# Loading q in memory order, half B first in the last batch, and norms placed by GpSimd's readiness: one change to a fused BigBird attention and FNet kernel

## The chip, the cores and the metric

The program runs on one core of a Trainium2 chip. The time is the device time of one launch in microseconds (us), given as the median of several executions. The span of a profiled execution is about 2 us shorter than its time; where the text takes numbers from the inside of a trace, it speaks of the span. In the traces PE is TensorE's matmuls and PEld its weight loads, DVE is VectorE, ACT ScalarE, POOL GpSimd and SP SyncE; SPq and ACTq are the queues of instructions of these engines, from which transfers are issued. PSUM is the memory that TensorE writes to. The granted clock is the share of TensorE's full clock that the trace recorded, 1.00 or 0.50 at any moment and a mean over a stretch.

## The reference, cut to what matters

Attention for 4 batches of 8 heads, 768 positions of 64 values each, under a block mask that is the same for all heads. Its output, as 768 rows of 512 per batch, goes through a two-dimensional Fourier mix, a normalisation of each row and two matrix products.

```python
scores = scale * np.matmul(q, k.transpose(0, 1, 3, 2))
...                                  # band, first/last block, three sampled blocks a row
attn = np.exp(scores - max); attn = attn / (sum + 1e-09)
x = attn @ v                         # (B, H, S, D) -> (B, S, H*D)
mixed = np.real(np.fft.fft(np.fft.fft(x, axis=1), axis=2))
u  = x + mixed
un = (u - mean(u)) / np.sqrt(var(u) + 1e-06)
out = u + np.maximum(un @ w_ch1, 0.0) @ w_ch2
```

## The kernel before

Heads are worked in 16 pairs, and each pair in six slots. In a slot TensorE computes two blocks of scores, ScalarE takes their exponentials, and TensorE multiplies the exponentials of the slot before with v. In between come the transposes of the next pair's q and k, the rounding of the weights (which arrive as 64-bit numbers in 32 chunks), and from the second batch on the matmuls of the batch before. Every engine executes its instructions in the order in which they were emitted.

The 768 positions are kept in an order that suits the Fourier mix: rows walk up and down in steps of two. `_ORDER` describes it, and `_rows` turns each entry of it into one or more pieces of a transfer. Before the change q was put into this order by the loads themselves, so that a pair needs 18 of them:

```python
    def load_q(dst, b, h, n, tiles=range(C), queues=None):
        queues = queues or [nc.sync]
        for t in tiles:
            if t < T:
                for p0, cnt, rows in _rows(q[b, h], t, ((S * D, n),)):
                    queues[0].dma_start(out=dst[p0:p0 + cnt, t, 0:n, :], in_=rows)
                continue
            for i in range(n):
                for p0, cnt, rows in _rows(q[b, h + i], t):
                    queues[i % len(queues)].dma_start(out=dst[p0:p0 + cnt, t, i, :], in_=rows)
```

A half of q (or k) is then transposed and copied out of PSUM by one instruction:

```python
    def turn(n, a, half):
        ...
        for c in range(T):
            nc.tensor.transpose(tp[:, c * P:(c + 1) * P], t[:, T * half + c, :, :], ident)
        if n == 0 and a == 0:
            nc.vector.tensor_copy(out=dst[:, half * HS:(half + 1) * HS], in_=tp[:, 0:HS])
        else:
            nc.scalar.copy(out=dst[:, half * HS:(half + 1) * HS], in_=tp[:, 0:HS])
```

At the end of a batch the halves A (0) and B (1) of the rows follow one another. Each tile of 128 rows is added by VectorE and stored; `_rows` gives two stores of 64 rows for the last tile of half A, and one of 2 x 64 rows for the last tile of half B:

```python
            nc.vector.tensor_tensor(out=x[:, m, :], in0=y, in1=x[:, m, :], op=ALU.add)
            for p0, cnt, rows in _rows(out[b], T * half + m):
                nc.sync.dma_start(out=rows, in_=x[p0:p0 + cnt, m, :])
    ...
        for half in range(2):
            rest += [lambda half=half, f=f: hidden(half, f) for f in range(NF)]
            rest += [lambda half=half, m=m, p=p: channels(half, m, p) ...]
```

A last part, `with tc.If(over > 0): general()`, is a slow way for large inputs. It is never executed with these inputs, but its branch is.

## Time and profile before

| what | kernel before |
|---|---|
| time, median of 3 runs | 1183.69 us |
| profiled span | 1180.5 us |
| TensorE busy | 1134.4 us |
| ScalarE busy | 364.8 us |
| issues of q loads by SyncE and by ScalarE | 278 and 10 (16 pairs of 18) |

Two more readings. First, the windows of slots 1 and 2. The columns are the stretch, its length, busy time (and count) of PE, PEld, DVE, ACT and POOL, the granted clock, DMA share and GB/s.

```profile
15.28:29.30 14.02, 8.75 (x32) 2.60 (x32) 0.56 (x1) 2.72 (x6) 0.00 (x0) 0.88 0.40 107
29.30:35.85 6.55, 6.55 (x31) 2.15 (x31) 3.79 (x7) 5.07 (x9) 0.00 (x0) 0.73 0.64 225
```

Second, the row of groups for the copies of q out of PSUM on ScalarE (busy us and mean ns behind the bar): 30 copies of 384 columns.

```profile
L448 ACT COPY qT<-tp 128x384 f32<-128x384 f32 x30 | 14.3, 478 | 65.3 <-PE tp L443 65.3
```

### The profile page before, as it was taken

What the parts mean: (1) busy time and instruction counts of PE and PEld (TensorE: products, weight loads), DVE (VectorE), ACT (ScalarE), POOL (GpSimd) and SP (SyncE); (2) the same over time, 40 slices, a digit from 0 to 9 for tenths busy, and PEclk for the clock granted to TensorE, in tenths of its full rate; (3) what the DMA queues carried; (4) which work ended last, traced back from release to release, by engine and by line L of the source; (5) the groups of instructions that cost most, each with busy time, mean ns of one, the idle gap of its engine ahead of it and who ended that gap; (6) DMA issues with size and microseconds to landing.
All of it is one profiled execution on the core that took longest, in us unless ns stands there. A gap on an engine that the chain in (4) does not pass through costs nothing.

```text
span 1180.5 us, 11884 instructions
## 1 busy us (share of the span) xinstructions
PE 1134.4 (96%) x4412; PEld 542.6 (46%) x4412; DVE 413.5 (35%) x751; ACT 364.8 (31%) x672; POOL 245.7 (21%) x181
## 2 busy tenths in 40 slices
PE   5999998989999999999999999999999999999996
PEld 1333333434654555455444555454444554554542
DVE  2787889487201433022224743022232223000000
ACT  1876765445200321144323331044321211100100
POOL 0000057457100311043333421033331001000000
PEclk9998999989999999999999999999999999999998
DMA  5546511111000100010101000001000000000000
GB/s 141 169 127 216 179 40 46 36 35 37 1 6 24 25 1 9 31 29 26 29 23 45 14 14 3 29 23 27 1 18 9 1 1 19 9 5 23 0 10 20
DMA packets 65281, 44.26 MB, mean 37 GB/s; under 512 B 52902, under 2 KB 58048, under 8 KB 65216
## 3 DMA queue, kind: packets, MB, share of 16 engines
q1 hardware_dynamic: 62576, 42.44, 12.6%
q10 hardware_dynamic: 2640, 0.98, 0.3%
q8 instruction: 37, 0.61, 0.2%
q14 instruction: 28, 0.23, 0.1%
HBM read 37.11 MB, written 6.29 MB: 37 GB/s over the span
## 4 chain that ended last, share of the span: by engine, by line
PE 88%; DVE 4%; ACT 2%; DMA 2%; issue 1%; SPq 1%; POOL 0%; ACTq 0%; DVEq 0%; POOLq 0%
PE hp L796 28%; PE y L810 28%; PE s L468 10%; PE o L510 9%; PE tp L443 2%; DVE e L489 2%; PE zp L670 1%; PE zp L681 1%; PE sp L557 1%; PE utp L786 1%; DMA qr<-in_q_dram 1%; PE xt L528 1%; PE s L473 1%; DMA wraw<-in_moe_w_ch_dram 1%; PE sp L571 1%
## 5 line engine op out<-in xcount | busy, mean ns | idle before, releaser
L796 PE MATMUL hp<-unT,w_sb 128*128 128x384 f32 x1024 | 341.4, 487 | 0.7 <-ACT unT L787 0.7
L810 PE MATMUL y<-w_sb,hs 128*128 128x512 f32 x768 | 337.6, 593 | 0.0
L796 PEld LDWEIGHTS hp<-unT,w_sb 128*128 128x128 f32 x1024 | 190.5, 190 | 131.1 <-issue 4.2
L498 POOL TENSOR_TENSOR acc<-acc,e 128x768 f32<-128x768 f32 x96 | 178.3, 1857 | 315.4 <-DVE e L489 311.2
L810 PEld LDWEIGHTS y<-w_sb,hs 128*128 128x128 f32 x768 | 142.8, 190 | 169.6 <-issue 168.6
L489 DVE TENSOR_TENSOR e<-s,mask 128x768 f32<-128x768 f32 x144 | 131.1, 951 | 249.5 <-ACT s L487 249.5
L468 PE MATMUL s<-qT,kT 64*128 64x384 f32 x768 | 165.5, 538 | 14.6 <-ACT e L484 8.0
L798 ACT ACTIVATE hs<-hp 128x384 f32<-128x384 f32 x128 | 62.7, 490 | 357.9 <-PE hp L796 357.9
L510 PE MATMUL o<-e,vr 128*64 128x384 f32 x768 | 149.5, 511 | 0.0
L487 ACT ACTIVATE s<-s 128x768 f32<-128x768 f32 x144 | 108.8, 793 | 91.4 <-PE s L468 90.7
L815 DVE TENSOR_TENSOR x<-y,x 128x512 f32<-128x512 f32 x24 | 16.6, 691 | 336.3 <-PE y L810 336.3
L468 PEld LDWEIGHTS s<-qT,kT 64*128 64x128 f32 x768 | 65.4, 192 | 76.2 <-issue 31.1
L496 POOL TENSOR_TENSOR acc<-e 128x768 f32<-128x768 f32 x24 | 44.5, 1856 | 268.2 <-DVE e L489 206.3
L510 PEld LDWEIGHTS o<-e,vr 128*64 128x64 f32 x768 | 47.6, 139 | 77.8 <-issue 74.3
L484 ACT ACTIVATE e<-s 128x768 f32<-128x768 f32 x48 | 36.6, 803 | 19.9 <-DMA qk<-in_q_dram 11.3
L745 POOL TENSOR_SCALAR rstd<-mv 128x1 f32<-128x1 f32 x24 | 6.4, 267 | 152.8 <-DVE mv L743 152.1
L712 DVE TENSOR_TENSOR un<-pq,un 128x255 f32<-128x255 f32 x12 | 5.1, 423 | 88.3 <-ACT un L709 88.3
L787 ACT COPY unT<-utp 128x512 f32<-128x512 f32 x24 | 14.0, 585 | 68.9 <-PE utp L786 68.8
L448 ACT COPY qT<-tp 128x384 f32<-128x384 f32 x30 | 14.3, 478 | 65.3 <-PE tp L443 65.3
L731 DVE TENSOR_TENSOR x<-x,un 128x127 f32<-128x127 f32 x96 | 32.7, 402 | 0.1
L443 PE MATMUL tp<-ident,qr 128*128 128x128 f32 x90 | 18.6, 307 | 9.0 <-DVE sums L541 3.5
L448 ACT COPY kT<-tp 128x384 f32<-128x384 f32 x32 | 15.3, 479 | 32.7 <-PE tp L443 30.1
(142 smaller groups left out, 680.3 us busy)
## 6 DMA issues: line engine op xcount, KB each, us to landing
wraw<-in_moe_w_ch_dram SPq DMA_DIRECT2D x32, 512.0 KB
vr<-in_v_dram SPq DMA_DIRECT2D x30, 192.0 KB
kr<-in_k_dram SPq DMA_DIRECT2D x28, 192.0 KB
qr<-in_q_dram SPq DMA_DIRECT2D x118, 32.0 KB
out_dram<-x SPq DMA_DIRECT2D x16, 128.0 KB
out_dram<-x SPq DMA_DIRECT2D x8, 256.0 KB
qr<-in_q_dram SPq DMA_DIRECT2D x59, 31.5 KB
out_dram<-x SPq DMA_DIRECT2D x8, 126.0 KB
```

The source lines that it names most:

```text
L443: nc.tensor.transpose(tp[:, c * P:(c + 1) * P], t[:, T * half + c, :, :], ident)
L468: nc.tensor.matmul(s[:, i, 0:HS], kT[D * i:D * i + D, c * P:(c + 1) * P], qT[D * i:D * i + D, half * HS:(half + 1) * HS], start=True, stop ...
L484: nc.scalar.activation(out=e, in_=s[:, :, 0:HS], func=ACT.Exp, scale=scale)
L487: nc.scalar.activation(out=s[:, :, 0:HS], in_=s[:, :, 0:HS], func=ACT.Exp, scale=scale)
L489: nc.vector.tensor_tensor(out=e, in0=s[:, :, 0:HS], in1=m.broadcast_to([P, 2, HS]), op=ALU.mult)
L496: nc.gpsimd.tensor_add(out=acc_of[n, half], in0=e_of[u - 1], in1=e)
L498: nc.gpsimd.tensor_add(out=acc_of[n, half], in0=acc_of[n, half], in1=e)
L510: nc.tensor.matmul(o[D * i:D * i + D, :], vt[:, i, c, :], e[:, i, :], start=(c == 0), stop=(c == C - 1))
L731: tt(out=xs, in0=xs, in1=at, op=op)
L796: nc.tensor.matmul(ps[:, 0:T * P], w1_sb[:, d, f * P:(f + 1) * P], unT[half][:, d, :], start=(d == 0), stop=(d == ND - 1))
L798: nc.scalar.activation(out=hs[half, f // 4][:, f % 4, :], in_=ps[:, 0:T * P], func=ACT.Relu)
L810: nc.tensor.matmul(y, hs[half, f // 4][:, f % 4, m * P:(m + 1) * P], w2_sb[:, f, :], start=(f == 0), stop=(f == NF - 1))
```

## The change

It has three parts. q is loaded as it lies in memory, two neighbouring rows to a partition, in 6 loads a pair (96 in all); the copies out of PSUM, now nine a pair, put it in order. The last batch works half B before half A, so that the tile with two plain stores comes last. And a normalisation on VectorE is placed by the scheduler only once GpSimd's reciprocal deviation should be there (`rstd_at`). With the first part, the sampled blocks are loaded by GpSimd in place of SyncE, some loads at the start move, and the transposes of the second pair's q come one slot earlier.

```diff
+_TURNED = (((0, 64, 192, -64, 64, 1), (256, 64, 256, -192, 64, 1), (129, 63, 385, -384, 63, 1),
+            (128, 127, 0, 384, 1, 1), (641, -128, 383, 127, 63, -1), (512, 127, 320, 191, 1, 1)),
+           ((384, 64, 191, 64, 64, -1), (704, -128, 64, 63, 63, -1), (640, 127, 0, 1, 1, 1)))
 ...
+        for t in range(T):
+            for i in range(2):
+                rows = q[b, 2 * j + i][2 * P * t:2 * P * (t + 1), :]
+                nc.sync.dma_start(out=qt[:, t, :, i, :],
+                                  in_=rows.rearrange("(p r) d -> p r d", r=2))
 ...
-    nc.sync.dma_start(out=samp_i.rearrange("a b c -> a (b c)"),
+    nc.gpsimd.dma_start(out=samp_i.rearrange("a b c -> a (b c)"),
 ...
+            copy = nc.vector.tensor_copy if n == 0 else nc.scalar.copy
+            for to, to_jump, frm, jump, cnt, step in _TURNED[half]:
+                copy(out=_grid(dst, to, 2, to_jump, cnt, 1),
+                     in_=_grid(tp, frm, 2, jump, cnt, step))
 ...
+            rstd_at.append(busy("POOL", 0.8, when["DVE"] + HOP) + HOP)
 ...
+                if kind == "w" and rstd_at[0] > max(when["DVE"], when["PE"]) + 0.2:
+                    break
 ...
+        order = (1, 0) if b == B - 1 else (0, 1)
 ...
-        for half in range(2):
+        for half in order:
 ...
-            for at, a, half in (((2, 0, 0), (3, 0, 1), (4, 1, 0), (5, 1, 1)) if n == 0 else
-                                ((1, 0, 0), (2, 0, 1), (4, 1, 0), (5, 1, 1))):
+            for at, a, half in ((1, 0, 0), (2, 0, 1), (4, 1, 0), (5, 1, 1)):
 ...
-        if sl == 0:
-            load_q_half(1, 1, [nc.sync, nc.scalar])
-        if s == (4 if n == 0 else 3) and n + 2 < len(pairs):
-            load_q_half(n + 2, 0)
-            load_q_half(n + 2, 1)
+        if s == 3 and n + 2 < len(pairs):
+            load_q(n + 2)
 ...
+    load_q(1)
     w_load(1)
     load_k(1)
-    load_q_half(1, 0)
-    w_load(2)
 ...
-    load_q_half(0, 1, [nc.sync, nc.scalar])
```

## The prediction

> **What bounds the kernel now.** I read the engine totals and the slices first.
>
> ```profile
> PE 1134.4 (96%) x4412; PEld 542.6 (46%) x4412; DVE 413.5 (35%) x751; ACT 364.8 (31%) x672; POOL 245.7 (21%) x181
> ...
> PE   5999998989999999999999999999999999999996
> ...
> PEclk9998999989999999999999999999999999999998
> ```
>
> TensorE is busy 1134.4 of 1180.5 us, so a change that removes no matmul can win only from the 46.1 us in which TensorE is idle, and from matmuls run at a reduced clock. The table of windows says where the idle time is: 0 to 12 us has 4.39 busy, 12 to 40 has 22.01, 40 to 140 has 94.43, 140 to 280 has 125.47, 280 to 320 has 38.19; then 320 to 1100 is fully busy at clock 1.00, and 1100 to 1181 has 69.91. So nothing between 320 and 1170 us can be gained; the case is decided in the first 320 us and in the last 10.
>
> Second, the list of what TensorE waited for:
>
> ```profile
> PE s L468 <- ACT e L484: 8.0, 3, 4.4
> PE tp L443 <- DMA qr<-in_q_dram: 7.0, 3, 5.4
> PE s L468 <- DVE e L489: 5.6, 6, 1.9
> PE xt L528 <- ACT oT L516: 4.0, 5, 1.0
> PE tp L443 <- DVE sums L541: 3.5, 1, 3.5
> ```
>
> The largest is a wait for ScalarE's exponentials, so third, the timeline shows why ScalarE was late. Twice the cause is the loading of q:
>
> ```profile
> 23.43 4.90 ACTq L199 DMA_DIRECT2D qk<-in_q_dram  x5
> ...
> 28.43 1.51 ACT L484 ACTIVATE e<-s 128x768 f32<-128x768 f32 x2 [11.30 <-DMA qk<-in_q_dram]
> 29.29 0.51 PEld L468 LDWEIGHTS s<-qT,kT 64*128 64x128 f32 x4 [4.58 <-ACT e L484]
> 29.30 1.65 PE L468 MATMUL s<-qT,kT 64*128 64x384 f32 x4 [4.39 <-ACT e L484]
> ```
>
> ScalarE issues five loads of q (23.43 to 28.33) in front of two exponentials whose scores were finished by 19.4; TensorE sits idle 4.39 us, and comes back slow (four score matmuls take 1.65 us; they take 0.92 from 35.9 on).
>
> ```profile
> 84.22 6.03 SPq L199 DMA_DIRECT2D qr<-in_q_dram  x10
> ...
> 90.36 1.63 SPq L402 DMA_DIRECT2D wraw<-in_moe_w_ch_dram  x3
> ...
> 94.98 0.66 ACT L411 ACTIVATE wraw<-wraw 128x512 f32<-128x512 uint32 x1 [4.31 <-DMA wraw<-in_moe_w_ch_dram]
> ...
> 98.22 1.65 PE L468 MATMUL s<-qT,kT 64*128 64x384 f32 x4 [2.88 <-ACT e L484]
> ```
>
> Here SyncE spends 79.28 to 90.25 issuing 18 loads of q (8, then these 10), and the weights queue behind them. ScalarE, which works in order, waits 4.31 us for the weight chunk with exponentials behind it, and TensorE waits 2.88. The slots from 90.0 and 98.2 took 8.2 us each where their neighbours take 5.0 to 5.2, with a granted clock of 0.62 in the second: 16.4 - 10.3 = 6.1 us lost in all.
>
> Last, the end. VectorE's last add ends at 1170.64, the span at 1180.5. By windows of one microsecond (DMA share and GB/s are the last two columns):
>
> ```profile
> 1088.00:1089.00 1.00, 1.00 (x5) 0.60 (x4) 0.16 (x1) 0.00 (x0) 0.00 (x0) 1.00 0.00 0
> 1089.00:1090.00 1.00, 1.00 (x5) 0.60 (x4) 0.00 (x0) 0.00 (x0) 0.00 (x0) 1.00 0.67 154
> 1090.00:1091.00 1.00, 1.00 (x5) 0.60 (x4) 0.00 (x0) 0.49 (x1) 0.00 (x0) 1.00 0.51 115
> ...
> 1173.00:1174.00 1.00, 0.00 (x0) 0.00 (x0) 0.00 (x0) 0.00 (x0) 0.00 (x0) 0.50 0.15 37
> ...
> 1177.00:1178.00 1.00, 0.00 (x0) 0.00 (x0) 0.00 (x0) 0.00 (x0) 0.00 (x0) 0.50 0.13 49
> ```
>
> Both are 256 KB of output. The last tile of half A (two stores of 64 rows) is through about 2.9 us after its add ended at 1088.16; the last of half B (one store of 2 x 64 rows) needs to about 1178.2, 7.6 us, at a DMA share of 0.13 to 0.16, that is two of sixteen engines.
>
> **What the Trainium skill says.** "DMA: Bandwidth & Descriptors", section "Why a DMA increments its semaphore by 16 and not by 1": a transfer uses the largest number of engines up to 16 that divides the slowest dimension of both sides. A destination of 2 x 64 rows gets 2, 64 or 128 rows get 16. The trace agrees: 0.13 to 0.16 is 2/16 and a little. The same holds for the q loads of tiles 3 to 5, and single rows get one engine. Same page, "Issuing engines are not separate DMA queues": issuing from another engine saves only the sequencer's time; here ScalarE's sequencer is the one that pays, 0.98 us a load. "ScalarE: Activation LUTs", "What ACT_TABLE_LOAD costs": an activation costs a fixed 186 ns plus 0.833 ns a column, and neighbours overlap by about 93 ns. The trace is some 28 ns below it: copies of 384, 126 and 2 columns take 478, 263 and 162 ns, and neighbours overlap by 0.1 us. "TensorE: Matmul & The Clock Gate", "What's actually happening": an idle window halves the clock and sustained work restores it. The slices at 26 to 31 us with clock 0.50, and the 1.65 us at 98.22, agree; why the dense stretch from 15.3 to 24 us ran at the slow durations too, the trace does not tell.
>
> **The change part by part.** I also compared the built instruction orders of the two kernels, engine by engine.
>
> *q loads.* 18 issues a pair become 6, all of 128 partitions. At about 0.6 us each (5.00/8, 5.67/10) a pair takes 3.7 us of SyncE for 10.9, and ScalarE issues no q. The weights behind them go out 7 us sooner, more than the 4.31 waited at 90.7, so the 6.1 us there are gained whole.
>
> *The start.* The first scores (9.62) get later. The sampled blocks are now loaded by GpSimd, ahead of its mask work; about 1 us (estimate, from the "~1 µs" first-byte figure for that path in the DMA page's "Specifications", since no GpSimd load is in this trace) delays the mask chain on VectorE, which ends at 9.07. Then VectorE does six copies in place of one: four of about 0.29 (0.558 less 256 columns) and two of 0.15, overlapping, 1.15 us for 0.56. First scores about 11.2. But slot 0 no longer waits for ScalarE (0.73 before), and slot 1 ends near 24.0, as before (24.9). At its end the order has four transposes of pair 1, whose six copies ScalarE must finish before the two of pair 0 can take the only bank: 1.2 + 1.0 wait + 0.5. Slot 2 scores at 26.7 in place of 29.3, 2.6 us won; the clock, not halved by a gap of over 4 us, should give about 0.7 more (0 to 3.4 is possible). The tight transpose after an output transpose near 41 us is moved: 0.5. Sum of the start: 3.8 us.
>
> *Copies out of PSUM.* ScalarE's two copies a pair (0.96 us) become nine: six large at 0.265 and three small at 0.162, 2.08 busy. Over 15 pairs that is +17 us of ScalarE's busy time, 365 to about 382. After overlap the first half costs 0.9 in place of 0.48, the second about 0.5 as before. ScalarE has 1.7 to 1.9 us to spare in the slots that hold the first half (2.99 and 3.16 busy of 4.9 from 127.4 to 137.2), so it is hidden, except where both halves of q are transposed back to back: TensorE's two waits for qT of 0.57 at 166.5 and 259.7 grow by 0.5 each: -1.0.
>
> *Half B first in the last batch.* The last tile is then two stores of 64 rows: 7.6 becomes 2.9, gain 4.7.
>
> *Norms.* In the built orders VectorE's normalisations stand where they stood in batches 0 to 2, and TensorE's order differs by one group of four matmuls. The waits this was meant for (2.34 us for GpSimd at 253.15, behind the 3.55 at 258.19) stay: 0.
>
> Sum: 6.1 + 3.8 + 4.7 - 1.0 = 13.6 us; 1183.69 - 13.6 = 1170.1.
>
> **Rivals.** (1) *ScalarE becomes the bound of the first stage*: the copies go into slots in which ScalarE is already tight (5.29 of 5.9 us from 121.5, 5.32 of 6.0 from 137.2, where TensorE loses 0.97). For it: an in-order engine, 1.1 us more a pair. Against: those slots hold the cheap second half. It would give back about 0.5 us in each of 15 pairs at most, only 8 of them where TensorE is not saturated: 4 us, 1174. (2) *The start is lost, not won*: GpSimd's load is slow or lands late and the mask chain ends several microseconds later. The scores then start at 13 or more and the gain of the start is gone: 1174. (3) *The clock comes up early*: with no gap after the first scores, slots 1 and 2 run warm (slot 1 took 8.2 us of matmuls; its warm work is 4.9), 3.4 us more: 1167. (4) *The norm rule works after all* and removes the 3.5 us at 258: 1167. Against it, the identical order.
>
> **Range and chances.** 1170 us; the terms at 90 us and at the end are read off the trace to a microsecond, the start is uncertain by 3 either way, the rivals by 4. So 1165 to 1176. A 2% gain would need 1160, that is 23.7 us, half of all idle time, and the roughly 16 us between 140 and 320 are not addressed: 0.04. Slower by 2% would need a new stall of over 37 us: 0.01.
>
> **What would show it.** Right: last add to end of span about 5 us; no wait for weights over 2 us before 110 us, and slots of 5.0 to 5.3 there; no q issues by ScalarE; TensorE's work from 320 us on moved as a block. Wrong: first scores after 12 us; ScalarE's exponentials late in the slots with the six copies; the 3.5 us at 258 gone; a tail still near 10 us.

## The result, and the profile after

The changed kernel takes 1164.34 us, median of four runs (1163.42 to 1167.2), beside 1184.41 us of the kernel before on the same chip. The ratio is 0.9834 with a 95% interval of 0.9812 to 0.9856. A ratio here is the mean time of one kernel's runs over that of the other's runs of the same rounds, so it is not quite the ratio of the medians. The predicted 1170 is 5.7 us too long, and the median lies 0.7 us under the low end of the range. Four later executions of the same file, on another occasion, took 1166.31 to 1168.3 us, inside it.

The totals and the clock of the kernel after:

```profile
PE 1124.9 (97%) x4412; PEld 540.4 (47%) x4412; DVE 414.4 (36%) x758; ACT 373.0 (32%) x777; POOL 247.1 (21%) x182
...
PEclk9999999989999999999999999999999999999999
```

The matmuls are the same 4412, so 9.5 us less of busy TensorE is the same work, less of it at the half clock (the mean granted clock over the span goes from 0.987 to 0.994). The rest of the 18.8 us of span is idle time removed, and ScalarE pays 8.2 us for it.

A span can be cut at marks that exist in both traces: the start of slot 4 (its first scores), one transpose of attention output (at 142.66 us before), the first matmul of the hidden layer (`hp`), the end of VectorE's last add, and the end. The table gives each stretch in us, from the timelines of both kernels and of five runs described below.

| profiled run | to slot 4 | slot 4 to the transpose | to the first `hp` | to the end of the last add | tail | span |
|---|---|---|---|---|---|---|
| before | 41.99 | 100.67 | 151.87 | 876.1 | 9.9 | 1180.5 |
| after | 32.81 | 94.80 | 151.86 | 876.1 | 6.1 | 1161.7 |
| after, repeated | 35.09 | 94.75 | 154.32 | 876.1 | 6.1 | 1166.4 |
| q part alone | 35.01 | 94.80 | 154.36 | 876.1 | 9.4 | 1169.7 |
| half B first alone | 41.35 | 100.80 | 151.76 | 876.1 | 6.2 | 1176.2 |
| norms alone | 42.74 | 97.62 | 154.01 | 876.1 | 9.9 | 1180.4 |
| q in 18 pieces | 37.58 | 100.74 | 152.45 | 876.1 | 6.1 | 1173.0 |

Between before and after the stretches differ by 9.2, 5.9, 0, 0 and 3.7 us, in all 18.8. The stretch to the first `hp` takes 151.8 to 154.4 us with and without the change, and the next is always the same; neither belongs to it. (By the clock record the three runs at 151.8 to 151.9 had 10.2 us at half clock in that stretch, those at 154.0 to 154.4 had 13.7 to 17.1.)

The start first. The windows of slots 1 and 2 of the kernel after answer to the two shown of before:

```profile
15.94:23.07 7.13, 6.01 (x35) 2.26 (x35) 0.00 (x0) 4.03 (x12) 0.00 (x0) 1.00 0.99 333
23.07:27.89 4.82, 4.82 (x32) 1.64 (x31) 3.06 (x8) 4.58 (x8) 0.00 (x0) 1.00 0.17 63
```

Slot 1 takes 7.13 us in place of 14.02 and slot 2 takes 4.82 in place of 6.55. How that comes about is in the timeline of TensorE (start, duration, and the idle time before with its releaser):

```profile
11.08 1.65 PE L474 MATMUL s<-qT,kT 64*128 64x384 f32 x4 [2.90 <-DVE qT L452]
...
15.94 1.46 PE L474 MATMUL s<-qT,kT 64*128 64x384 f32 x4
...
17.59 0.92 PE L474 MATMUL s<-qT,kT 64*128 64x384 f32 x4
...
22.70 0.44 PE L444 MATMUL tp<-ident,qr 128*128 128x128 f32 x2 [1.12 <-ACT qT L452]
23.07 0.92 PE L474 MATMUL s<-qT,kT 64*128 64x384 f32 x4
```

Four score matmuls take 1.65 us, then 1.46, then 0.92: the clock rises to full about 17 us, 6 us after the first scores, and stays there. In the kernel before, the same groups still take 1.65 us at 29.30, and 0.92 only from 35.85 on. (One trap: in the windows the clock reads 1.00 before the first change that the trace has recorded, though the matmuls there run at the slow duration. At the start of a trace, read the durations.) Of the wait of 1.12 us at 22.70 the prediction had said 1.0.

Near 70 us SyncE now spends 3.85 us on the q loads of a pair, and the weights follow at 74.38:

```profile
70.44 3.85 SPq L214 DMA_DIRECT2D qr<-in_q_dram  x6
...
74.38 1.49 SPq L400 DMA_DIRECT2D wraw<-in_moe_w_ch_dram  x3
```

ScalarE's rows for the copies, by form, hold nine copies a pair where the row of before held two:

```profile
L452 ACT COPY qT<-tp 128x126 f32<-128x126 f32 x45 | 12.3, 274 | 0.0
...
L452 ACT COPY qT<-tp 128x128 f32<-128x128 f32 x45 | 10.5, 269 | 63.7 <-PE tp L444 63.7
...
L452 ACT COPY qT<-tp 128x2 f32<-128x2 f32 x45 | 7.8, 174 | 0.5
```

They sum to 30.6 us where 14.3 were before, 16.3 more (17 predicted), of which 8.2 remain as busy time because neighbours overlap. In the list of what TensorE waited for, the waits for these copies did grow, and the wait for VectorE's sums is still there:

```profile
PE xt L534 <- ACT oT L522: 4.1, 5, 1.0
...
PE tp L444 <- DVE sums L547: 3.6, 1, 3.6
PE tp L444 <- ACT qT L452: 3.4, 3, 1.1
```

Last the tail. VectorE's last add ends at 1155.56. The windows of one microsecond show the two stores of 64 rows running at a share of 0.85, and the rows of the line that closes the program show what SyncE did meanwhile (duration in ns min/median/max, then first and last start):

```profile
1157.00:1158.00 1.00, 0.00 (x0) 0.00 (x0) 0.00 (x0) 0.00 (x0) 0.00 (x0) 0.56 0.85 195
1158.00:1159.00 1.00, 0.00 (x0) 0.00 (x0) 0.00 (x0) 0.00 (x0) 0.00 (x0) 0.50 0.08 23
```

```profile
L1114 SPq COMPARE_BRANCH  x1: 50/50/50, 1156.8 to 1156.8; - x1
...
L1114 SPq EVENT_SEMAPHORE  x8: 17/17/17, 1159.7 to 1160.2; - x8
```

The data is through about 2.7 us after the add, as predicted (2.9). But SyncE's branch over the unused slow way, begun at 1156.8, lets the next instruction start only at 1159.7: 2.9 us, and that now comes last.

### The profile page after: what moved, and what is told of

Read it like the earlier page. It is cut to its first block, busy times and chain, and to the rows that moved or that the text cites. A ratio compares the mean times of both kernels' runs of the same rounds, so it can differ in the third digit from the quotient of the medians.

```text
span 1161.7 us, 11697 instructions
## 1 busy us (share of the span) xinstructions
PE 1124.9 (97%) x4412; PEld 540.4 (47%) x4412; DVE 414.4 (36%) x758; ACT 373.0 (32%) x777; POOL 247.1 (21%) x182
## 4 chain that ended last, share of the span: by engine, by line
PE 91%; DVE 4%; ACT 2%; issue 1%; POOL 0%; ACTq 0%; POOLq 0%; DVEq 0%
PE hp L808 29%; PE y L822 29%; PE s L474 11%; PE o L516 10%; PE tp L444 2%; DVE e L495 1%; PE zp L676 1%; PE zp L687 1%; PE sp L563 1%; PE s L479 1%; PE xt L534 1%; PE utp L798 1%; PE sp L577 1%; DVE x L737 0%; PE pq L696 0%
## 5 line engine op out<-in xcount | busy, mean ns | idle before, releaser
L474 PE MATMUL s<-qT,kT 64*128 64x384 f32 x768 | 162.4, 529 | 8.9 <-DVE e L495 5.8
L516 PE MATMUL o<-e,vr 128*64 128x384 f32 x768 | 145.9, 501 | 0.0
L452 ACT COPY qT<-tp 128x128 f32<-128x128 f32 (+1 forms) x135 | 22.4, 239 | 64.2 <-PE tp L444 63.7
```

Of the source, the lines that this page charges most:

```text
L474: nc.tensor.matmul(s[:, i, 0:HS], kT[D * i:D * i + D, c * P:(c + 1) * P], qT[D * i:D * i + D, half * HS:(half + 1) * HS], start=True, stop ...
L516: nc.tensor.matmul(o[D * i:D * i + D, :], vt[:, i, c, :], e[:, i, :], start=(c == 0), stop=(c == C - 1))
```

## The experiments

Twelve more runs were made, one of them of the unedited kernel after; all gave correct results. They are told in the order of what they settle.

**The three parts alone.** `q part alone` is the kernel after with the old order of halves and the old norm rule. `Half B first alone` and `norms alone` are the kernel before with one part each.

```diff
# q part alone, against after
-        order = (1, 0) if b == B - 1 else (0, 1)
+        order = (0, 1)
-        wh = [[("w", lambda ...: whiten(half, m), 0.0, 0.0, 0.6) ...
+        wh = [[d(0.6, whiten, half, m) ...
# half B first alone, against before
+        order = (1, 0) if b == B - 1 else (0, 1)
-        for half in range(2):
+        for half in order:
# norms alone, against before
+            rstd_at.append(busy("POOL", 0.8, when["DVE"] + HOP) + HOP)
+                if kind == "w" and rstd_at[0] > max(when["DVE"], when["PE"]) + 0.2:
+                    break
```

> The changed kernel with the first half leading in every batch and the norms placed by the old rule, so the q part alone. Theory A (the gain is the q loads: start 9.3 us, weights near 90 us 5.8 us, read off the two traces): 15 us below the kernel before, 1168 to 1170, the tail from the last add to the end back near 9.9 us. Rival B (the three parts need each other, the norm rule carries part of the middle): 1172 or more.

> The kernel before with half B leading in the last batch and nothing else. Theory A (the tail is the store over two engines, and under it lies SyncE's branch of 2.9 us, so 3.7 us are won and not the predicted 4.7): 1180 to 1181, last add to end 6.1 us, the first 320 us as before. Rival B (the tail is other work, for instance the end of the program): no change, 1184.

> The kernel before with the norm rule alone. Theory A (VectorE's order is the same, so nothing moves): within 1 us of the kernel before, and the wait of 3.5 us for the sums near 258 us stays. Rival B (the rule carries part of the gain in the first 320 us): 1 to 3.5 us faster and that wait shorter.

Measured, beside 1183.23 us of the kernel before: q part 1169.49 us (ratio 0.9869, 0.9843 to 0.9895), half B first 1177.84 (0.9949, 0.9923 to 0.9974), norms 1182.26 (0.999, 0.9959 to 1.0021). The table of stretches shows where: the q part has the two early gains and the long tail, half B first has the short tail and neither of the early gains. Norms alone keeps the whole wait that it was meant for; its line in the waits of TensorE:

```profile
PE tp L443 <- DVE sums L541: 3.5, 1, 3.5
```

So the gain is the q part's and the tail's, and the norm rule gives nothing that these runs resolve. By the medians the parts give 13.7 and 5.4 us, 19.1 in sum; the whole gave 20.1 the first time and 15.7 when it was repeated (below), so that they add up is not contradicted, and not shown more closely than that. Half B first was some 2 us faster than expected; its trace shows 3.7 us in the tail, and the kernel before alone spread from 1180.27 to 1187.69 in these rounds.

**q in 18 pieces.** The kernel after, with the same bytes in the same places but each load cut in three by partitions, brings back the number of issues and nothing else.

```diff
-                nc.sync.dma_start(out=qt[:, t, :, i, :],
-                                  in_=rows.rearrange("(p r) d -> p r d", r=2))
+                rows = rows.rearrange("(p r) d -> p r d", r=2)
+                for p0, p1 in ((0, 48), (48, 96), (96, 128)):
+                    nc.sync.dma_start(out=qt[p0:p1, t, :, i, :], in_=rows[p0:p1])
```

> The changed kernel with each load of q cut into three by partitions (48, 48, 32): 18 issues a pair again, the same bytes and packets, all on 16 engines. Theory A (the weights were late because SyncE spent 11 us issuing q ahead of them): ScalarE's wait for weights comes back, one or two slots over 6 us between 60 and 110 us, 4 to 8 us slower than the changed kernel, 1168 to 1172. Rival B (the weights waited behind q's packets on the two engines that carried them): no such wait, within 1.5 us of the changed kernel.

Measured: 1173.93 us, ratio 0.9912 (0.9888 to 0.9936). The stretch from slot 4 to the transpose is 100.74 us, that of the kernel before, where after has 94.80. Its timeline of SyncE and its list of waits give the chain:

```profile
74.68 11.48 SPq L216 DMA_DIRECT2D qr<-in_q_dram  x18
...
86.26 1.48 SPq L401 DMA_DIRECT2D wraw<-in_moe_w_ch_dram  x3
```

```profile
ACT wraw L410 <- DMA wraw<-in_moe_w_ch_dram: 9.5, 4, 3.8
...
PE s L475 <- ACT e L491: 4.3, 2, 2.7
```

Eighteen issues hold SyncE for 11.48 us, so the weights go out 11.6 us after the first of them and not 3.9; ScalarE waits 3.8 us for a chunk, and TensorE waits 2.7 us for ScalarE and comes back with score groups of 1.65 us. So the count of issues, for the same bytes, brings the 5.9 us back. About half of them is the wait, the other half the slow clock behind it, and the second half need not come: in norms alone, which has the old loads, TensorE waited nearly as long, the clock stayed up, and the stretch took 97.62 us, only 2.8 more than in the kernel after. The first line is from q in 18 pieces, the second from norms alone:

```profile
93.72 1.65 PE L475 MATMUL s<-qT,kT 64*128 64x384 f32 x4 [2.70 <-ACT e L491]
```

```profile
98.79 0.92 PE L468 MATMUL s<-qT,kT 64*128 64x384 f32 x4 [2.61 <-ACT e L484]
```

The time is 2 us over the expected 1168 to 1172: another 2.5 us come at the start, where slot 4 begins at 37.58, not near 35: slot 3 waits 1.63 us for an exponential. This run does not say more of the start.

**The kernel after once more, and the start.** Before the start could be judged, the spread between executions of the same file had to be known.

```diff
# after, repeated: no edit
```

> The changed kernel once more, unedited, beside the variants of this call. It should repeat: 1163 to 1168 us, in two groups some 3 us apart if the moment at which the clock comes up (17 us in its first profile, about 22 in the profile of the q part alone) is what differs between executions.

Measured: 1167.3 us, ratio 0.9861 (0.9839 to 0.9882), against 0.9834 the first time; two groups, as expected, do not show in these four executions. The timeline of TensorE shows what differs at the start:

```profile
15.95 1.65 PE L474 MATMUL s<-qT,kT 64*128 64x384 f32 x4
...
17.96 1.65 PE L474 MATMUL s<-qT,kT 64*128 64x384 f32 x4
...
25.35 0.92 PE L474 MATMUL s<-qT,kT 64*128 64x384 f32 x4
```

The first scores are at 11.09 us, where they were the first time, but the clock rises only after 19.6, by the clock record near 22 us, not 17, so slot 2 starts 2.3 us later, by an event that the program does not order. Taking the first profile as the value of the change overstates it: slot 4 starts at 32.81, 35.09, 35.01 and 35.74 us in the profiled runs with the new start (after twice, q part alone, and the run without the branch below), 34.7 on average; and at 41.99, 41.35, 42.74 and 42.70 in those with the old one (before, half B first, norms, and the warmed kernel before below), 42.2 on average. The start is worth about 7.5 us, not 9.2, and 3.8 had been predicted.

**Is it the clock, or the loads?** Two runs give TensorE something to do before the first scores, transposes of the identity into an unused bank, so that the clock is up early. In the kernel before, 10 and 4 of them; in the kernel after, 10 and 14.

```diff
+    def warm(n):
+        tp = ps_m.tile([P, 512], FP32, tag="m", name="warm")
+        for _ in range(n):
+            nc.tensor.transpose(tp[:, 0:P], ident, ident)
+    warm(10)
     turn(0, 1, 0)
     turn(0, 0, 0)
+    warm(14)      # the kernel before: warm(10) ahead of the two turns, warm(4) behind
```

> The kernel before with 14 idle transposes ahead of the first scores. Theory A (in the kernel before the loads of q hold the start, and the half clock hides behind them; the gap of 4 us takes the clock away again): slots 0 and 1 get shorter, but slot 2 still starts at 28 to 29.5 after ScalarE's q issues, with slow matmuls; at most 1.5 us faster. Rival B (the slow clock alone held the start): 4 us or more faster.

> The changed kernel with 24 idle transposes of the identity on TensorE before the first scores, which nothing reads: 10 ahead of the first transpose of k, 14 after those of q. Theory A (the extra gain of the start is that the clock came up early and stayed; it comes up when TensorE has been busy long enough): full clock by the first scores, slots 0 and 1 in about 2.8 + 5 us where they took 4.9 + 7.1, so slot 3 some 3 us earlier than at 27.9, 1161 to 1163, and less spread. Rival B (slots 0 and 1 are held by loads and copies and not by the clock): within 1 us of the changed kernel.

Measured, beside 1182.74 us: the warmed kernel before 1181.22 us (0.9978, 0.9952 to 1.0004), the warmed kernel after 1161.14 us (0.982, 0.9794 to 0.9846). In the kernel after the four score matmuls take 0.92 us from the first at 11.12 on, and slot 4 starts at 30.16; in time its ratio is not clear of the kernel after's 0.9834 and 0.9861. In the kernel before the extra transposes did not bring the clock up: its score groups take 1.65 us at 11.66, 19.18 and 31.02, and slot 2 still waits, 3.48 us for the exponentials behind ScalarE's loads of q. So that run does not answer how a warm kernel before would start. It only shows that this much early work doesn't help while the gaps remain.

The opposite experiment puts the gap into the kernel after: two long copies on ScalarE at the end of slot 1, into weights that aren't there yet (5.52 us).

```diff
+    def hold(n):
+        for _ in range(n):
+            nc.scalar.copy(out=w2_sb[:, 0:6, :]..., in_=ident[:]...broadcast_to([P, 24, P]))
 ...
         w_steps(sl)
+        if sl == 1:
+            hold(2)
```

> The changed kernel with two copies of 3072 columns (some 5.3 us) put into ScalarE's order ahead of the exponentials of slot 2, as the five q issues stood in the kernel before. Theory A (a hold of ScalarE there costs its own length and, by an idle TensorE, the clock of the following slot): TensorE idles 4 to 5 us before the scores of slot 3, then four score matmuls take 1.65 us again; slot 3 starts near 32.4 in place of 27.9, slot 4 near 39 in place of 32.8; 4.5 to 7.5 us slower in all. Rival B (later slack of TensorE takes it up): under 2 us slower.

Measured: 1174.62 us, ratio 0.9927 (0.9904 to 0.995). Its timeline and the window of its slot 3, and below it the window of slot 3 in the kernel after:

```profile
35.52 1.65 PE L474 MATMUL s<-qT,kT 64*128 64x384 f32 x4 [4.60 <-ACT e L490]
...
35.52:44.34 8.82, 8.82 (x32) 2.62 (x32) 3.40 (x6) 4.94 (x11) 0.00 (x0) 0.52 0.53 150
```

```profile
27.89:32.81 4.92, 4.92 (x32) 1.74 (x31) 4.71 (x9) 4.23 (x10) 0.00 (x0) 1.00 0.47 127
```

One gap of 4.60 us costs itself and then 3.9 us more, because the whole next slot of unchanged work runs at a clock of 0.52. A gap of the same kind and size, 4.39 us, is what the change removed. In this run the gap cost 8.5 us, nearly twice its length. (The kernel after was not run in the same rounds. Slot 4 comes at 44.34, not near 39 as expected, also because the clock came up late, at 23.55, so that slot 2 began at 26.03.) In the start of the kernel before, the clock record has the rise at 22.6 us and the fall at 26.0, in the middle of its gap, and the next rise at 32.8: it lost the clock in the same way. That this accounts for the whole difference of the averages is inferred.

The clock records of all fourteen profiled runs say more about when a gap costs the clock (windows on both sides of a change give its moment). Within each trace all changes of the clock are whole multiples of 3.41 us apart, and where these steps lie relative to the program differs from execution to execution. Every step at full clock in which TensorE was busy for less than half was followed by half clock, none in which it was busy for more than 0.61 was, and between these both occurred; the half clock then lasted one, two or three steps. So where a gap lies in the steps matters too: the gap of 2.70 us of q in 18 pieces lay in a step that was 0.21 busy, that of 2.61 us of norms alone was spread over two that were 0.66 and 0.58 busy, and cost no clock. The prediction spoke of an idle window that halves the clock; a step need not be idle throughout, as the fall ahead of 98.22 us in the kernel before came at the end of one that was 0.32 busy.

**An earlier mask chain.** The delay of the first scores (9.62 to 11.08 us) was the cost foreseen at the start. Here the sampled blocks are loaded by SyncE again, and a spreading of the mask is moved behind the first transposes.

```diff
-    nc.gpsimd.dma_start(out=samp_i.rearrange("a b c -> a (b c)"),
+    nc.sync.dma_start(out=samp_i.rearrange("a b c -> a (b c)"),
-    spread_q(keep_q[0:NB, :], keep)
 ...
     turn(0, 0, 0)
+    spread_q(keep_q[0:NB, :], keep)
```

> The changed kernel with the sampled blocks loaded from SyncE again and the spread of the second mask operand, which no score needs, moved behind the first copies of q on VectorE. Theory A (after the change VectorE's mask chain sets the first scores; GpSimd's load delays it by 1.1 us, the second spread by 1.7): first scores near 8.9 to 9.5 in place of 11.08, 1162 to 1163.5. Rival B (the q loads set the first scores): first scores stay over 10.5, no change.

Measured: 1166.29 us (1161.92 to 1166.58), ratio 0.986 (0.9837 to 0.9883). The first scores come at 9.33 us, 1.75 earlier than in the kernel after, and slot 4 at 31.19. But three of the four executions are at 1166.3 to 1166.6, among those of the unedited kernel, and only the profiled one is at 1161.92. The place is shown, a gain in time is not.

**Are the copies hidden, and by how much?** Every copy of q out of PSUM on ScalarE is done twice.

```diff
-                copy(out=_grid(dst, to, 2, to_jump, cnt, 1),
-                     in_=_grid(tp, frm, 2, jump, cnt, step))
+                for _ in range(1 if n == 0 else 2):
+                    copy(out=_grid(dst, to, 2, to_jump, cnt, 1),
+                         in_=_grid(tp, frm, 2, jump, cnt, step))
```

> The changed kernel with each of ScalarE's copies of q out of PSUM made twice (135 more, about +22 us of ScalarE's busy time), the instruction order on TensorE unchanged. Theory A (the copies are hidden but where both halves of q are transposed back to back): at the three places TensorE's wait grows by about 1 us, the rest is slack; 0 to 3 us slower. Rival B (ScalarE is at its limit in the first 140 us, every added copy shows): 5 us or more slower.

Measured: 1184.88 us, ratio 1.0015 (0.9982 to 1.0049), 17.6 us over the kernel after of the same rounds. The waits of TensorE:

```profile
PE tp L444 <- ACT qT L453: 9.5, 4, 2.7
...
PE xt L535 <- ACT oT L523: 8.2, 7, 2.2
```

These two rows are 17.7 us where the kernel after has 7.5 (3.4 and 4.1, shown above): 10.2 more, and after gaps of 2.2 to 2.7 us the work is slow again (69.0 to 74.5 us at a clock of 0.54 by the windows). The size is that of rival B, not the 0 to 3 us expected. The one copy is hidden, and the same copy again is not: ScalarE's slack in the first 320 us, after the change, did not hold another set of these copies. How much less it would have held was not measured. The rival "ScalarE becomes the bound" was not what happened with one set.

**The branch at the end.** The slow way and its branch are taken out. That kernel is right for these inputs only.

```diff
-            over = nc.values_load(flag[0:1, 0:1], min_val=0, max_val=1)
+            pass
 ...
-    with tc.If(over > 0):
-        general()
```

> The changed kernel without the closing branch and the fallback behind it (right for these inputs only). Theory A (the last microsecond of the predicted tail gain is lost because SyncE, after its last store, spends 2.9 us on the taken branch, longer than the stores now need): last add to end about 5 us in place of 6.1, some 1 us faster. Rival B (the end waits for the stores' receipts): the tail stays 6.1.

Measured: 1164.78 us, ratio 0.9846 (0.9825 to 0.9867), beside 1167.3 of the unedited kernel. The last add ends at 1158.52 and the span at 1162.3, a tail of 3.8 us where the branch leaves 6.1. So 2.3 us of the tail are the branch's, where 1 had been expected. Without it the tail would be 6.1 us shorter than before, more than the 4.7 predicted; with it, 3.7.

**A kernel that takes what these runs showed.** The kernel after with the earlier mask chain, early transposes (14 and 8), the kernel before's places for the transposes of pair 1, and the second of the last two stores issued by ScalarE.

```diff
+    warm(14)
     turn(0, 1, 0)
     turn(0, 0, 0)
+    warm(8)
+    spread_q(keep_q[0:NB, :], keep)
 ...
-            for at, a, half in ((1, 0, 0), (2, 0, 1), (4, 1, 0), (5, 1, 1)):
+            for at, a, half in (((2, 0, 0), (3, 0, 1), (4, 1, 0), (5, 1, 1)) if n == 0 else
+                                ((1, 0, 0), (2, 0, 1), (4, 1, 0), (5, 1, 1))):
 ...
+            end = b == B - 1 and half == 0 and m == T - 1
-                nc.sync.dma_start(out=rows, in_=x[p0:p0 + cnt, m, :])
+                (nc.scalar if end and i else nc.sync).dma_start(out=rows, in_=...)
```

> The changed kernel with four edits together: the sampled blocks from SyncE and the second mask operand spread later; 22 idle transposes ahead of the first scores; the first half of pair 1's q turned one slot later; the very last store issued by ScalarE. From the single runs: first scores near 9.3 (-1.7), full clock from there (-2.7), a wait of 1.1 gone, 0.5 at the end: 1158 to 1160 us, less spread. If the parts don't add (the mask chain or the loads bind again) 1161.

Measured: 1159.49 us (1157.3 to 1159.93), ratio 0.9793 (0.9774 to 0.9811). It beats both kernels, by 23.5 us and by 7.8 us in the same rounds; whether it is faster than the kernel before by the full 2% is unclear by the interval. The scores start at 9.55 us at nearly the full clock, and slot 4 at 28.40, where the kernel after had 35.09 in that call. The tail is 5.7 us, 0.4 less than after.

## Why the prediction was right or wrong

The median was missed by 5.7 us, in the direction of a larger gain. Step by step:

- **What bounds the kernel.** Right. From the first `hp` to the last add, 876.1 us, nothing moved in any run; all of the gain lies before and behind it.
- **The weights near 90 us, 6.1 us.** Right: 5.9 measured, and the cause (18 issues ahead of the weights) is shown by putting the 18 issues back. There is some luck in the size: half of it is a fall of the clock, which the prediction took over from one profile. It came in four of the five profiled kernels with 18 issues at that place; in norms alone, without it, the term would have been 2.8 us.
- **The start, 3.8 us.** This is the step that failed, and in it the term for the clock. Its other pieces were right where they were read off the trace: first scores at 11.08 us (11.2 predicted), a wait of 1.12 us for the six copies (1.0), no q issues on ScalarE. What failed is "slot 1 ends near 24.0, as before" together with the "about 0.7 more" for the clock after it. The prediction itself said that the trace did not tell why slot 1 was slow, took its slow duration over, and gave little for the work behind it. In the first profile the clock came up inside slot 1, and the work ahead of its four transposes ended at 20.93 us. In the other three profiled runs with the new start it ended at 23.1 to 23.9, not far from the 24.0. But in all four, slots 2 and 3 ran at the full clock: 9.74 us from the start of slot 2 to that of slot 4, where 11.5 had been allowed (12.69 before, less 0.7 and 0.5). The start gave 9.2 us in the first profile and 7.5 on average over the profiled runs; about half of the 3.7 us above the prediction lie in slots 2 and 3. This is the third rival, "the clock comes up early", which was to be worth 3.4 us more. The rival was named and sized, and then not taken into the middle of the estimate.
- **Copies out of PSUM, -1.0 us.** The waits grew as said, by about half a microsecond at each of the two places, but the stretch that holds them took 151.86 us beside 151.87: no loss shows. By the windows TensorE's 725 matmuls there were busy 1.2 us less (136.49 and 135.25 us), about what the waits grew; as the same kernel repeated took 154.32 us there, a term of 1 us can't be resolved by one pair of profiles. ScalarE's total went to 373 us, not 382, because the prediction added up the copies without their overlap.
- **Half B first, 4.7 us.** The mechanism is right (data through 2.7 us behind the add, 2.9 predicted), the size is 3.7, because the branch of SyncE then comes last. The prediction compared the last tile with one in the middle of the kernel, and there no branch follows.
- **Norms, 0.** Right, by norms alone and by the wait of 3.6 us that stays.
- **Rivals.** "ScalarE becomes the bound" did not happen, but with every copy made twice the kernel lost 17.6 us. "The start is lost" did not happen. "The norm rule works after all" did not happen.

The sum by the first pair of profiles: 13.6 predicted, plus 5.4 for the start, less 0.2 for the weights, plus 1.0 for the copies, less 1.0 for the tail, is 18.8 us.

What stays open is why the clock rises 6 us after the first scores in one execution and 11 to 12 in others of the same start (4 in the run with the copies made twice). The steps of 3.41 us alone do not decide it: in the repeated run TensorE was busy throughout three whole steps before the rise at 22.05, in the first profile throughout one. This moves the start of slot 4 between 32.81 and 35.74 us, and so the size of the miss: the eight timed executions of the changed kernel lie between 1163.4 and 1168.3 us.

## What to carry to other kernels

Work that ran slow behind a gap should be predicted at its full-clock duration when a change removes the gap, as slots 2 and 3 did here in all four runs. A stretch that is slow for a reason that the trace does not tell should be given the whole range between the two durations (slot 1's work ahead of its transposes ended at 20.93 us in one run and at 23.1 to 23.9 in three). A gap in TensorE's work can cost the clock of the work behind it: the one of 4.60 us put in here cost 8.5 us. So loads that hold up an in-order engine can be worth more than the wait that the profile shows for them. When the last transfer is made short, look at what else the last engines still do (here a branch), and when an engine is said to hide some work, ask by how much: a second helping of the same copies cost 17.6 us, more than the q part had won.

## What the Trainium skill lacked or had wrong

- "TensorE: Matmul & The Clock Gate", section "What you observe", puts the change to the fast clock around 4 us into sustained work, plus or minus 0.5 us from run to run. Here the same program, at work without a gap from 11.08 us on, got the full clock near 17 us in one execution and after 19.6 us (near 22 by the clock record) in another: 6 and 11 us. So a slow stretch of that length need not be a sign of gaps. Behind the gap of 4.60 us, too, the return took longer: a slot of 8.82 us without a gap ran at a mean clock of 0.52.
- "DMA: Bandwidth & Descriptors", section "Issuing engines are not separate DMA queues", calls the time to issue a transfer usually small relative to the transfer. Here 18 issues took 11.48 us of SyncE, and their number, for the same bytes, made 5.9 us of the span in that run (2.8 would be left where the clock stays up, by norms alone).
- "Runtime: NRT & Kernel Launch", section "Instruction fetch mechanics", says that a taken branch to a target outside the window forces a fetch, and gives no duration. The trace shows 2.9 us on SyncE between the branch and the next instruction; without the branch the tail is 2.3 us shorter. In these 2.9 us the record of the DMA queues has two packets of instructions, and without the branch none in the last 7 us. That it is this fetch which takes the time is still inferred.
